# Dense-weight conversion in pairs of blocks: one 1024-column operation where two of 512 columns stood

## The chip, the cores and the metric

The kernel runs on one core of one Trainium2 chip. The time is the device time of one execution in microseconds, taken as the median of three runs.

## The reference

Three layers follow each other on 2304 tokens (4 sequences of 576) of width 512:

```
scores = q @ k.T / sqrt(64)           # 8 heads, causal, window of 64 keys
attn   = softmax(where(mask, scores, -1e9)); x = attn @ v
h = max(x @ w_in, 0);  x = (h * h) @ w_out        # dense: 512 -> 2048 -> 512
e = argmax(x @ w_gate); g = softmax(x @ w_gate)[e]  # 8 experts, one for each token
out = g * (max(x @ w1[e], 0) @ w2[e])             # 512 -> 1024 -> 512
```

In the program the two dense weight arrays `w_in` and `w_out` arrive as 64-bit words, two 32-bit words for each element; the kernel makes fp32 numbers of them.

## The kernel before

Matrix products are made of three products each: a number is kept as a high part (rounded to TensorE's fp32r format) and a low part (the rest), and `mm3` adds high by high, high by low and low by high (lines 168 to 170).

The dense layer works on 9 slices `st` of 256 tokens and 16 chunks `f` of 128 hidden columns. `gemm1(st, f)` makes a chunk's hidden values, `hidden` (ScalarE, L464), `square` (ScalarE L471, VectorE L473) and `square_low` (VectorE, L480) turn them into the parts `gh` and `gl`, and `gemm2(st, f)` adds them to the slice's output. A list `order` gives the pairs (st, f): slices 0 and 1 interleaved first, then slice after slice. Attention (`att_scores` to `att_out`) runs ahead, in blocks `g` of 64 tokens; the first eight blocks take their maxima straight from PSUM (L377) and scale them in a second operation (L380), before ScalarE's exponentials (L398).

The dense weights are converted while slices 0 and 1 run. A chunk f has two blocks of 128 x 512 elements, n = 2f from `w_in` and n = 2f+1 from `w_out`. The steps are:

- `load_w(n)` issues the DMA of one block (512 KB) from SyncE's queue into a ring `stg` of four buffers.
- `conv_a(f)`: ScalarE takes the absolute value of the upper words of each block (L186) into a ring `tmp` of four.
- `conv_b(f)`: four steps on VectorE for each block: clamp (L203), shift and mask (L205), merge with the sign and exponent bits (L207), merge with the lower word's bits (L211). Then it asks for the blocks of chunk f + 2.
- `conv_c(f)`: for each block ScalarE makes the high part (L228), and VectorE or GpSimd the low part (L230): VectorE every third block, GpSimd the others.

A table of slots says when each step is emitted; the order within an engine's queue in the dense part comes out of a planner that simulates the program with its own costs. After the dense part the experts' weights go through the same `stg` buffers (`wload`, `wsplit`), and each expert is one group of products.

Of the kernel before, what the change touches and what calls it, by code (L numbers as in the profile page):

```python
# [11 lines left out]
F32 = mybir.dt.float32  # L12
F32R = mybir.dt.float32r
BF16 = mybir.dt.bfloat16
I32 = mybir.dt.int32
U32 = mybir.dt.uint32
ACTF = mybir.ActivationFunctionType
ALU = mybir.AluOpType
AX = mybir.AxisListType
P = 128  # L20


def word(bits):

    return struct.unpack("<f", struct.pack("<I", bits))[0]
# [24 lines left out]
def kernel(  # L50
# [13 lines left out]
    nc = tc.nc  # L64
    B, _, NB, W, HP = qT.shape
# [3 lines left out]
    E, _, F1 = w1.shape  # L69
# [13 lines left out]
    SCALE = 1.0 / math.sqrt(D)  # L83
# [4 lines left out]
    cpool = ctx.enter_context(tc.tile_pool(name="cpool", bufs=1))  # L88
# [4 lines left out]
    bpool = bpool_ctx.__enter__()  # L93
# [3 lines left out]
    cr = Ring(cpool)  # L97
    br = Ring(bpool)
# [6 lines left out]
    kring = epool.tile([P, 4, HP, W], F32, tag="k", name="k")  # L105
    xhl = [epool.tile([P, KD, 3 * ST], F32R, tag=f"x{p_}", name=f"x{p_}") for p_ in "hl"]

    br.make([P, 512], I32, "tmp", 4)
    for p_ in "hl":
        br.make([P, ST], F32R, f"g{p_}", 3)  # L110

# [7 lines left out]
    for half in range(2):  # L119
# [5 lines left out]
            out=mid, in_=mid, pattern=[[-1, P]], compare_op=ALU.is_ge, fill=NEG, base=W, channel_multiplier=1  # L125
# [33 lines left out]
    def wunit():  # L159
        return cr.tile([P, 4096], F32R, "w", 4)  # L160
# [12 lines left out]

    wi_u, wo_u, wst = {}, {}, {}

    def stage():
        return cr.tile([P, 1024], F32, "stg", 4)


    conv = {}  # L180

    def conv_a(f):
        for n in (2 * f, 2 * f + 1):
            w = wst.pop(n).rearrange("p (n two) -> p n two", two=2)
            c = br.tile([P, 512], I32, "tmp", 4)
            nc.scalar.activation(c.bitcast(F32), w[:, :, 1].bitcast(F32), ACTF.Abs)  # L186
            conv[n] = w[:, :, 0], w[:, :, 1], c

    def conv_b(f):
        half, fo = divmod(f, NF // 2)  # L190
        if f == NF // 2:
            fpool_ctx.__exit__(None, None, None)
            wpool = ctx.enter_context(tc.tile_pool(name="wpool", bufs=1, side="right"))
            cr.tiles["w"] += [wpool.tile([P, 4096], F32R, tag=f"w{i}", name=f"w{i}") for i in range(4, 8)]
        if fo == 0:
            for p_ in "hl":
                wi_u[half, p_] = wunit().rearrange("p (k f) -> p k f", k=KD)
                wo_u[half, p_] = wunit().rearrange("p (f d) -> p f d", d=DM)
        two = [conv.pop(2 * f + i) for i in range(2)]

        for _, _, c in two:
            cf = c.bitcast(F32)
            nc.vector.tensor_scalar(cf, cf, word(0x38100000), word(0x47EFFFFF), op0=ALU.max, op1=ALU.min)  # L203
        for _, _, c in two:
            nc.vector.tensor_scalar(c, c, 3, 0x3FFFFFFF, op0=ALU.logical_shift_left, op1=ALU.bitwise_and)  # L205
        for _, high, c in two:
            nc.vector.scalar_tensor_tensor(  # L207
                out=c, in0=high, scalar=-(1 << 30), in1=c, op0=ALU.bitwise_and, op1=ALU.bitwise_or
            )
        for low, _, c in two:  # L210
            nc.vector.scalar_tensor_tensor(  # L211
                out=c, in0=low, scalar=29, in1=c, op0=ALU.logical_shift_right, op1=ALU.bitwise_or
            )
        conv[f, "c"] = two
        for n in (2 * f + 4, 2 * f + 5):
            if n < 2 * NF:
                load_w(n)

    def conv_c(f):
        half, fo = divmod(f, NF // 2)  # L220
        for which, (_, _, c) in enumerate(conv.pop((f, "c"))):
            c = c.bitcast(F32)
            if which:
                h, l = (wo_u[half, p_][:, fo, :] for p_ in "hl")
            else:
                h, l = (wi_u[half, p_][:, :, fo * P:(fo + 1) * P] for p_ in "hl")
                c = c.rearrange("p (k f) -> p k f", k=KD)
            nc.scalar.copy(h, c)  # L228
            low = nc.vector if (2 * f + which) % 3 == 2 else nc.gpsimd
            low.tensor_tensor(l, c, h.bitcast(F32), op=ALU.subtract)  # L230

    def load_w(n):
        f, which = divmod(n, 2)
        wst[n] = stage().bitcast(I32)
        if which:
            nc.sync.dma_start(wst[n], w_out[f * P:(f + 1) * P, :])
        else:
            nc.sync.dma_start(
                wst[n].rearrange("p (k f) -> p k f", k=KD),
                w_in[:, 2 * f * P:2 * (f + 1) * P].rearrange("(k p) f -> p k f", p=P),  # L240
            )
# [3 lines left out]
    wsp, stg, busiest, done = {}, {}, [], {}  # L245
# [127 lines left out]
    def att_max(g):  # L373
        ps = probs[g]
        if g < NE:
            nmax = br.tile([P, HP], F32, "nmax", 3)
            nc.vector.tensor_reduce(  # L377
                out=nmax, in_=ps.rearrange("p (h k) -> p h k", h=HP), axis=AX.X, op=ALU.max, negate=True
            )
            nc.vector.tensor_scalar_mul(nmax, nmax, SCALE)  # L380
            probs[g] = ps, nmax
            return
        s = er.tile([P, HP, P], F32, "s", 3)
        m = mask[:, 0 if g % NB else 1, :].unsqueeze(1).to_broadcast([P, HP, P])
        nc.vector.scalar_tensor_tensor(
            out=s, in0=ps.rearrange("p (h k) -> p h k", h=HP), scalar=SCALE, in1=m, op0=ALU.mult, op1=ALU.min
        )
        nmax = br.tile([P, HP], F32, "nmax", 3)
        nc.vector.tensor_reduce(out=nmax, in_=s, axis=AX.X, op=ALU.max, negate=True)
        probs[g] = s, nmax  # L390
# [463 lines left out]
    nc.vector.tensor_copy(ident_b, ident)  # L854
    nc.vector.tensor_scalar_min(mask_b, mask, 0.0)
    load_w(0)
    load_w(1)
    load_q(2, 2)
    load_k(2, 2)
# [35 lines left out]
    def chain(i, stages, x, gaps, most=2):  # L895
# [8 lines left out]
        return i  # L904

    ATT = (att_scores, att_max, att_exp, att_norm, att_transpose, att_evac, att_values, att_out)
    at(16, load_gates, 0)

# [6 lines left out]
    for f in range(NF):  # L915
        i = max(-3, min(f - 1, slot[0, f] - 2))
        at(i, conv_c, f)
        at(i - 1, conv_b, f)
        if f + 1 < NF:
            at(i - 1, conv_a, f + 1)  # L920
# [6 lines left out]
    for g in range(2 * QB, NS * QB):  # L927
        st, j = divmod(g, QB)
        i = slot[st, 0] - 19 + 4 * j
        if st == 2:  # L930
            i = slot[st, 0] - 13 + 2 * j
# [9 lines left out]
    for i in range(8):  # L941
# [3 lines left out]
        at(last + 8 + i, wload, *((-1, i + 4) if i < 4 else (0, i - 4)))  # L945

    conv_a(0)
    for i in range(-PRE, len(order) + LA):
        run(i, False)
# [5 lines left out]
        if i >= LA:  # L955
            st, f = order[i - LA]
# [200 lines left out]
```

## Time and profile before

| | |
|---|---|
| median of 3 runs | 841.28 us (840.61 to 845.0) |
| the profiled execution | 844.22 us, its span 842.5 us |
| PE busy | 789.9 us (94%) |
| DVE busy | 546.4 us (65%) |
| ACT busy | 400.6 us (48%) |
| POOL busy | 254.6 us (30%) |

PE is TensorE (PEld its weight loads), DVE is VectorE, ACT is ScalarE, POOL is GpSimd, SP is SyncE. Busy times are sums over instructions of one engine. The span is what the trace covers; the profiled execution's own time lies 1.7 us above it. The profiled execution is one of its own, beside the three runs.

### The profile page before, as it was taken

The numbers are of one execution on the slowest core, as the hardware profiler recorded it, in microseconds if no ns is written. First come the engines' busy times: TensorE is split into PE (matmuls) and PEld (weight loads), VectorE is DVE, ScalarE is ACT, GpSimd is POOL, SyncE is SP. The second block draws the span as 40 slices with busy tenths as digits, with TensorE's granted clock in tenths as the row PEclk, the third lists the DMA queues.
The fourth block names the chain that finished last, engine by engine and source line by source line (L and its number), as shares of the span: only waits on it lengthen the run. The fifth ranks groups of instructions, "written<-read, shape, count | busy, mean of one in ns | idle before, by whom it ended". The sixth has DMA issues, their size and how long they took to land.

```text
span 842.5 us, 15052 instructions
## 1 busy us (share of the span) xinstructions
PE 789.9 (94%) x5212; PEld 685.0 (81%) x5212; DVE 546.4 (65%) x1275; ACT 400.6 (48%) x1059; POOL 254.6 (30%) x257
## 2 busy tenths in 40 slices
PE   6888788999999999999999998989999999999894
PEld 5766667988889888889888897878798888888783
DVE  6999996795773946748558478557778654534110
ACT  6986654343443434344443435436677553433211
POOL 5425431112221122211211006164567642320201
PEclk9999999999999999999999999989999999999998
DMA  9854653110211212111110036366667654420101
GB/s 272 278 148 150 200 154 110 38 39 26 82 32 39 66 36 77 32 45 62 40 51 27 26 100 202 126 213 185 205 205 250 220 154 146 124 91 2 50 2 42
DMA packets 50861, 91.51 MB, mean 109 GB/s; under 512 B 8220, under 2 KB 24604, under 8 KB 50752
## 3 DMA queue, kind: packets, MB, share of 16 engines
q1 hardware_dynamic: 44688, 80.43, 30.3%
q0 software_dynamic: 6064, 9.63, 3.4%
q8 instruction: 69, 1.13, 0.5%
q14 instruction: 40, 0.33, 0.1%
HBM read 84.59 MB, written 13.81 MB: 117 GB/s over the span
## 4 chain that ended last, share of the span: by engine, by line
PE 64%; issue 14%; DVE 11%; DMA 6%; ACT 2%; POOL 2%; SPq 0%; POOLq 0%; DVEq 0%; ACTq 0%
PE h L168 10%; PE h L169 10%; PE h L170 10%; PE y L168 9%; PE y L170 9%; PE y L169 9%; DMA stg<-in_moe_w_out 2%; PE a L362 2%; DVE tmp L207 2%; DVE tmp L211 2%; PE a L435 2%; DVE tmp L203 1%; DMA stg<-in_moe_w 1%; PE a L685 1%; PE a L420 1%
## 5 line engine op out<-in xcount | busy, mean ns | idle before, releaser
L168 PE MATMUL h<-xh,w 128*128 128x256 f32 (+3 forms) x864 | 263.0, 305 | 18.4 <-DVE gl L480 14.2
L169 PE MATMUL h<-xl,w 128*128 128x256 f32 (+3 forms) x864 | 254.9, 295 | 0.4 <-DVE xl L997 0.4
L170 PE MATMUL h<-xh,w 128*128 128x256 f32 (+3 forms) x864 | 254.6, 295 | 0.0
L168 PEld LDWEIGHTS h<-xh,w 128*128 128x128 f32 x864 | 164.2, 190 | 37.9 <-DVE gl L480 19.5
L169 PEld LDWEIGHTS h<-xl,w 128*128 128x128 f32 x864 | 164.5, 190 | 8.1 <-DVE xl L997 0.6
L170 PEld LDWEIGHTS h<-xh,w 128*128 128x128 f32 x864 | 164.4, 190 | 2.8
L464 ACT ACTIVATE r<-h 128x256 f32<-128x256 f32 x144 | 55.2, 384 | 201.7 <-PE h L170 194.0
L168 PE MATMUL y<-w,gh 128*128 128x512 f32 x294 | 119.2, 406 | 4.0 <-ACT gh L471 3.9
L772 DVE SCALAR_TENSOR_TENSOR ggl<-h,ggh 128x512 fp32r<-128x512 f32 (+1 forms) x69 | 46.2, 669 | 114.2 <-ACT ggh L771 114.1
L169 PE MATMUL y<-w,gh 128*128 128x512 f32 x294 | 116.4, 396 | 0.0
L473 DVE SCALAR_TENSOR_TENSOR h<-h,r 128x256 f32<-128x256 f32 x144 | 61.3, 426 | 84.4 <-ACT r L464 84.4
L170 PE MATMUL y<-w,gl 128*128 128x512 f32 x294 | 102.3, 395 | 0.5 <-DVE gl L772 0.5
L771 ACT ACTIVATE ggh<-h 128x512 fp32r<-128x512 f32 (+1 forms) x69 | 40.3, 584 | 124.6 <-PE h L170 96.0
L550 DVE SCALAR_TENSOR_TENSOR tmp<-tmp,stg 128x512 f32<-128x512 f32 x128 | 95.6, 747 | 0.8
L336 POOL COPY q<-qd 64x256 f32<-64x256 f32 x46 | 33.5, 729 | 149.7 <-PE a L362 148.4
L168 PE MATMUL y<-w,ggh 128*128 128x512 f32 x170 | 70.8, 416 | 0.6 <-ACT ggh L771 0.6
L170 PE MATMUL y<-w,ggl 128*128 128x512 f32 x170 | 67.6, 398 | 1.4 <-DVE junk L998 1.1
L168 PEld LDWEIGHTS y<-w,gh 128*128 128x128 f32 x294 | 55.6, 189 | 15.4 <-ACT gh L471 6.0
L169 PE MATMUL y<-w,ggh 128*128 128x512 f32 x170 | 67.1, 395 | 0.0
L480 DVE TENSOR_TENSOR gl<-h,gh 128x256 fp32r<-128x256 f32 x144 | 60.4, 420 | 7.7 <-ACT gh L471 1.0
L278 POOL TENSOR_TENSOR w<-stg,w 128x512 fp32r<-128x512 f32 x27 | 36.4, 1354 | 91.6 <-ACT w L277 88.7
L169 PEld LDWEIGHTS y<-w,gh 128*128 128x128 f32 x294 | 55.6, 189 | 9.5
(165 smaller groups left out, 1276.1 us busy)
## 6 DMA issues: line engine op xcount, KB each, us to landing
stg<-in_moe_w SPq DMA_DIRECT2D x45, 512.0 KB, 4.1
stgx<-in_moe_w SPq DMA_DIRECT2D x18, 512.0 KB, 4.5
stg<-in_moe_w_in SPq DMA_DIRECT2D x16, 512.0 KB, 4.3
stg<-in_moe_w_out SPq DMA_DIRECT2D x16, 512.0 KB, 3.9
v<-in_v SPq DMA_DIRECT2D x28, 256.0 KB, 2.6
x_d<-tmp SPq DMA_DIRECT2D x18, 256.0 KB, 2.0
q<-in_moe_w SPq DMA_DIRECT2D x9, 512.0 KB, 4.7
qd<-in_q SPq DMA_DIRECT2D x28, 128.0 KB, 2.1
```

The lines of the kernel that those rows point to most:

```text
L168: nc.tensor.matmul(o, lhsT=ah, rhs=bh, start=first, stop=False)
L169: nc.tensor.matmul(o, lhsT=ah, rhs=bl, start=False, stop=False)
L170: nc.tensor.matmul(o, lhsT=al, rhs=bh, start=False, stop=last)
L207: nc.vector.scalar_tensor_tensor(out=c, in0=high, scalar=-(1 << 30), in1=c, op0=ALU.bitwise_and, op1=ALU.bitwise_or)
L278: rest.tensor_tensor(l[:, a:a + 512], src, h[:, a:a + 512].bitcast(F32), op=ALU.subtract)
L336: nc.gpsimd.tensor_copy(qk[g][rows, :, half, :], d[rows])
L464: nc.scalar.activation(r, gT[st, f][:, :ST], ACTF.Relu)
L473: nc.vector.scalar_tensor_tensor(out=ps[:, ST:2 * ST], in0=ps[:, :ST], scalar=0.0, in1=r, op0=ALU.max, op1=ALU.mult)
L480: nc.vector.tensor_tensor(gl, ps[:, ST:2 * ST], gh.bitcast(F32), op=ALU.subtract)
L550: nc.vector.scalar_tensor_tensor(out=junk, in0=x2sb[tt], scalar=1.0, in1=w, op0=ALU.mult, op1=ALU.mult, accum_out=l[:, t, e:e + 1])
L771: nc.scalar.activation(h[:, :width], hid[f][:, :width], ACTF.Relu)
L772: nc.vector.scalar_tensor_tensor(out=l[:, :width], in0=hid[f][:, :width], scalar=0.0, in1=h[:, :width].bitcast(F32), op0=ALU.max, op1=ALU. ...
```

## The change

The rings `tmp` and `stg` become pairs: two tiles of twice the size each, whose halves are the old four buffers. `conv_a` takes the absolute value of a chunk's two blocks in one operation of 1024 columns, and the four steps of `conv_b` are one operation each on 1024 columns. `conv_c` still works on the halves; of the low parts VectorE now makes every sixth (five of 32), GpSimd the others. The scaling of the first eight maxima goes from VectorE to ScalarE.

```
-    br.make([P, 512], I32, "tmp", 4)
+    tmp2 = [bpool.tile([P, 2, 512], I32, tag=f"tmp{i}", name=f"tmp{i}") for i in range(2)]
+    br.tiles["tmp"], br.at["tmp"] = [t[:, i] for t in tmp2 for i in range(2)], -1
+    stg2 = [cpool.tile([P, 2, 1024], F32, tag=f"stg{i}", name=f"stg{i}") for i in range(2)]
+    cr.tiles["stg"], cr.at["stg"] = [t[:, i] for t in stg2 for i in range(2)], -1
...
     def conv_a(f):
-        for n in (2 * f, 2 * f + 1):
-            w = wst.pop(n).rearrange("p (n two) -> p n two", two=2)
-            c = br.tile([P, 512], I32, "tmp", 4)
-            nc.scalar.activation(c.bitcast(F32), w[:, :, 1].bitcast(F32), ACTF.Abs)
-            conv[n] = w[:, :, 0], w[:, :, 1], c
+        i = (br.at["tmp"] + 1) % 4
+        assert i % 2 == 0
+        c = [br.tile([P, 512], I32, "tmp", 4) for _ in range(2)]
+        whole = tmp2[i // 2].rearrange("p t n -> p (t n)")
+        w = stg2[f % 2].bitcast(I32).rearrange("p t (n two) -> p (t n) two", two=2)
+        nc.scalar.activation(whole.bitcast(F32), w[:, :, 1].bitcast(F32), ACTF.Abs)
+        conv[f] = w[:, :, 0], w[:, :, 1], whole, c
...
-        two = [conv.pop(2 * f + i) for i in range(2)]
-        for _, _, c in two:
-            cf = c.bitcast(F32)
-            nc.vector.tensor_scalar(cf, cf, word(0x38100000), word(0x47EFFFFF), op0=ALU.max, op1=ALU.min)
...
+        low, high, c, _ = conv[f]
+        cf = c.bitcast(F32)
+        nc.vector.tensor_scalar(cf, cf, word(0x38100000), word(0x47EFFFFF), op0=ALU.max, op1=ALU.min)
+        nc.vector.tensor_scalar(c, c, 3, 0x3FFFFFFF, op0=ALU.logical_shift_left, op1=ALU.bitwise_and)
+        nc.vector.scalar_tensor_tensor(
+            out=c, in0=high, scalar=-(1 << 30), in1=c, op0=ALU.bitwise_and, op1=ALU.bitwise_or
+        )
+        nc.vector.scalar_tensor_tensor(
+            out=c, in0=low, scalar=29, in1=c, op0=ALU.logical_shift_right, op1=ALU.bitwise_or
+        )
...
-            low = nc.vector if (2 * f + which) % 3 == 2 else nc.gpsimd
+            low = nc.vector if (2 * f + which) % 6 == 5 else nc.gpsimd
...
-            nc.vector.tensor_scalar_mul(nmax, nmax, SCALE)
+            nc.scalar.mul(nmax, nmax, SCALE)
```

## Rows read from the trace of the kernel before

**Rows 1.** Stages: us, then busy us (instructions) by engine, clock, DMA share, GB/s

```profile
0.00:44.00 44.00, 32.98 (x265) 29.37 (x266) 36.72 (x83) 35.81 (x111) 21.19 (x38) 0.96 0.86 266
44.00:137.50 93.50, 75.91 (x520) 61.05 (x520) 92.09 (x176) 59.57 (x152) 36.02 (x28) 0.98 0.51 159
137.50:490.00 352.50, 352.50 (x2595) 312.96 (x2594) 226.88 (x700) 146.61 (x476) 67.02 (x78) 1.00 0.15 46
490.00:842.00 352.00, 328.47 (x1838) 281.63 (x1836) 190.71 (x320) 158.57 (x323) 130.34 (x114) 0.97 0.43 139
```

**Rows 2.** The chain that ended last, its shares by engine

```profile
PE 64%; issue 14%; DVE 11%; DMA 6%; ACT 2%; POOL 2%; SPq 0%; POOLq 0%; DVEq 0%; ACTq 0%
```

**Rows 3.** Waits from 44 to 137.5 us: total us, times, longest us

```profile
PEld h L168 <- DVE gl L480: 16.5, 17, 2.2
PE h L168 <- DVE gl L480: 12.6, 12, 1.8
...
ACT tmp L186 <- DMA stg<-in_moe_w_in: 5.8, 4, 4.6
...
ACT tmp L186 <- DMA stg<-in_moe_w_out: 4.7, 5, 1.5
...
ACT tmp L186 <- DVE w L230: 3.6, 3, 2.0
...
DVE tmp L203 <- ACT tmp L186: 1.4, 2, 0.9
```

**Rows 4.** VectorE's groups from 44 to 137.5 us: busy us, mean ns, idle before

```profile
L207 DVE SCALAR_TENSOR_TENSOR tmp<-stg,tmp 128x512 int32<-128x512 int32 x24 | 19.6, 819 | 0.0
L211 DVE SCALAR_TENSOR_TENSOR tmp<-stg,tmp 128x512 int32<-128x512 int32 x24 | 19.6, 816 | 0.0
L205 DVE TENSOR_SCALAR tmp<-tmp 128x512 int32<-128x512 int32 x24 | 16.8, 705 | 0.0
L203 DVE TENSOR_SCALAR tmp<-tmp 128x512 f32<-128x512 f32 x24 | 13.0, 542 | 1.4 <-ACT tmp L186 1.4
...
L230 DVE TENSOR_TENSOR w<-tmp,w 128x512 fp32r<-128x512 f32 x8 | 7.0, 872 | 0.0
```

**Rows 5.** VectorE in order of time from 63 us: start, duration

```profile
63.13 0.16 DVE L412 TENSOR_SCALAR tot<-tot 128x4 f32<-128x4 f32 x1
63.20 0.42 DVE L205 TENSOR_SCALAR tmp<-tmp 128x512 int32<-128x512 int32 x1
63.53 0.41 DVE L165 TENSOR_TENSOR xl<-a,xh 128x256 fp32r<-128x256 f32 x1
...
64.20 0.69 DVE L207 SCALAR_TENSOR_TENSOR tmp<-stg,tmp 128x512 int32<-128x512 int32 x1
64.80 0.42 DVE L480 TENSOR_TENSOR gl<-h,gh 128x256 fp32r<-128x256 f32 x1
```

**Rows 6.** GpSimd's groups from 44 to 137.5 us

```profile
L230 POOL TENSOR_TENSOR w<-tmp,w 128x512 fp32r<-128x512 f32 x16 | 23.1, 1446 | 40.6 <-ACT w L228 40.6
L414 POOL TENSOR_TENSOR s<-s,tot 128x512 f32<-128x512 f32 x6 | 7.7, 1278 | 11.3 <-DVE tot L413 11.2
L336 POOL COPY q<-qd 64x256 f32<-64x256 f32 x6 | 6.7, 1117 | 7.9 <-PE a L362 7.7
```

**Rows 7.** GpSimd in order of time near 81 us

```profile
80.73 1.49 POOL L414 TENSOR_TENSOR s<-s,tot 128x512 f32<-128x512 f32 x1
```

**Rows 8.** VectorE in order of time, beside rows 7

```profile
81.25 0.41 DVE L165 TENSOR_TENSOR xl<-a,xh 128x256 fp32r<-128x256 f32 x1
81.58 0.93 DVE L205 TENSOR_SCALAR tmp<-tmp 128x512 int32<-128x512 int32 x1
82.42 0.42 DVE L473 SCALAR_TENSOR_TENSOR h<-h,r 128x256 f32<-128x256 f32 x1
```

**Rows 9.** ScalarE's conversion groups, 44 to 137.5 us

```profile
L186 ACT ACTIVATE tmp<-stg 128x512 f32<-128x512 f32 x22 | 14.8, 674 | 16.6 <-DMA stg<-in_moe_w_in 5.8 <-DMA stg<-in_moe_w_out 4.7 <-DVE w L230 3.6
```

**Rows 10.** Loads of stg issued from 44 to 137.5 us, issue to landing

```profile
DMA to landing us min/median/max: 3.2/3.7/6.4
```

**Rows 11.** The scaling of the first eight maxima: ns min/median/max, first and last start

```profile
L380 DVE TENSOR_SCALAR nmax<-nmax x8: 155/158/999, 8.9 to 34.7; 128x4 f32<-128x4 f32 x8
```

More of the change, by code (lines that the diff above doesn't have):

```diff
@@ L174 @@
     wi_u, wo_u, wst = {}, {}, {}
-    def stage():
-        return cr.tile([P, 1024], F32, "stg", 4)
     conv = {}
     def conv_a(f):
-        for n in (2 * f, 2 * f + 1):
-            w = wst.pop(n).rearrange("p (n two) -> p n two", two=2)
-            c = br.tile([P, 512], I32, "tmp", 4)
-            nc.scalar.activation(c.bitcast(F32), w[:, :, 1].bitcast(F32), ACTF.Abs)
-            conv[n] = w[:, :, 0], w[:, :, 1], c
+        i = (br.at["tmp"] + 1) % 4
[5 more added lines that the diff above has]
+        conv[f] = w[:, :, 0], w[:, :, 1], whole, c
     def conv_b(f):
@@ L198, in conv_b @@
                 wo_u[half, p_] = wunit().rearrange("p (f d) -> p f d", d=DM)
-        two = [conv.pop(2 * f + i) for i in range(2)]
-        for _, _, c in two:
-            cf = c.bitcast(F32)
-            nc.vector.tensor_scalar(cf, cf, word(0x38100000), word(0x47EFFFFF), op0=ALU.max, op1=ALU.min)
[L204 to L214, printed above, removed]
+        low, high, c, _ = conv[f]
[8 more added lines that the diff above has]
+        )
         for n in (2 * f + 4, 2 * f + 5):
@@ L220, in conv_c @@
         half, fo = divmod(f, NF // 2)
-        for which, (_, _, c) in enumerate(conv.pop((f, "c"))):
+        for which, c in enumerate(conv.pop(f)[3]):
             c = c.bitcast(F32)
@@ L233, in load_w @@
         f, which = divmod(n, 2)
-        wst[n] = stage().bitcast(I32)
+        wst[n] = cr.tile([P, 1024], F32, "stg", 4).bitcast(I32)
         if which:
```

## The prediction

> **What bounds the kernel now.** I read the stages first, then the chain that ended last, then the waits of the one stage that the change touches, and last VectorE and GpSimd there in order of time.
>
> The stages [rows 1] show three regimes. From 137.5 to 490 us PE is busy for the whole 352.5 us: what arrives at its start late ends late, and nothing that VectorE or ScalarE does faster inside it matters. From 490 us on PE has 24 us of gaps, among the experts' groups, which the change doesn't touch. From 44 to 137.5 us VectorE is busy for 92.1 of 93.5 us, and PE only for 75.9: VectorE is the bound, and PE has 17.6 us of gaps to give back. These 93.5 us hold the conversion of 12 of the 16 chunks (24 instructions of each step [rows 4]), 7.8 us a chunk. Before 44 us loads are the pace: the DMA engines are busy for 86% at 266 GB/s, VectorE for 36.7 of 44 us.
>
> The chain agrees: VectorE holds 11% of the span, some 93 us, beside PE's 64% [rows 2]. In the waits PE's first product of a chunk and its weight load wait for L480, the low part of the hidden values, 12.6 and 16.5 us (much of it the same time) [rows 3]. L480 itself is short; it stands in VectorE's queue behind the conversions. So a microsecond less of VectorE work between 44 and 137.5 us should bring the fully busy stretch of PE forward by about a microsecond, and the end with it.
>
> In order of time one sees two things. First, a spacing: a 512-column clamp or shift takes 0.33 us from its start to the next, a merge of two operands 0.60 us, and an operation on 4 columns still takes 0.07 us [rows 5]. Second, a stall: GpSimd's L414 runs from 80.73 to 82.22 us [rows 7]; VectorE's L165, which reads PSUM, passes beside it in its usual 0.41 us, but the next operation, L205, which reads and writes SBUF alone, takes 0.93 us instead of 0.42 and ends 0.29 us after GpSimd [rows 8]. The conversions carry this all through: mean 0.819, 0.816, 0.705, 0.542 and 0.872 us [rows 4] against 0.69 and 0.42 undisturbed [rows 5]. Times the counts this is 3.1 + 3.0 + 6.8 + 2.9 + 1.5 = 17.3 us of stall in the stage, while GpSimd works for 23.1 + 7.7 + 6.7 = 37.5 us [rows 6].
>
> **The change, part by part.** The sum goes by the profiled execution (844.22 us) as a difference, and I put the difference on the median of the runs, 841.28 us; the profiled one lies 2.9 us above it, inside the spread of the three.
>
> *Merged steps on VectorE.* An operation of 1024 columns instead of two of 512 saves one fixed part, 0.07 us [rows 5]. From 44 to 137.5 us that is 12 chunks x 4 x 0.07 = 3.4 us, on the engine that bounds. The four earlier chunks save 1.1 us, and I count them as nothing: there the loads are the pace.
>
> *Low parts to GpSimd.* Five go over (n = 2, 8, 14, 20, 26), four of them in the stage. VectorE is rid of 4 x 0.60 = 2.4 us. GpSimd gets 4 x 1.446 = 5.8 us more [rows 6]; it has the room (36.0 of 93.5 us busy), but its work stalls VectorE. By busy time a low part's share of the stall is 23.1/37.5 x 17.3 / 16 = 0.67 us, and 0.81 if the copies L336 cost nothing. On that count moving is worth 4 x (0.67 - 0.60) = +0.3 us, so nothing. Against that, stalls need an SBUF operation next in VectorE's queue: the conversions are 104 of its 176 instructions [rows 1, 4], and after merging 52 of 124, 0.71 of the former share. If stalls fall like it, they are 17.3 x 43.3/37.5 x 0.71 = 14.2 us, 3.1 less, and with the 2.4 the gain is 5.5 us. Neither end is shown; I take about their middle, -2.6 us. The upper bound of the cost is a stall for GpSimd's whole operation: 4 x (1.446 - 0.60) = +3.4 us.
>
> The row shows GpSimd's operation holding up VectorE only from the first SBUF operation on [rows 7, 8]. The Trainium skill, page "SBUF — State Buffer", sections "SBUF: two separate sides" and "Summary: rules for kernel authors", says that the two share a port pair as an exclusive lock held for the whole instruction, that a VectorE operation in a two-port mode or with two SBUF inputs is blocked fully, and that one should schedule whichever is off the critical path. Taken at its full length it speaks against moving low parts, and the sum would be -3.4 + 3.4 + 1.4 = +1.4 us instead of -4.6; the mean stall above, about half of an operation, bears out the lock but not its full length.
>
> *The pair as the unit.* ScalarE's absolute value now needs both blocks landed and both halves of `tmp` free, VectorE's clamp needs all of it, and both loads of chunk f + 2 are asked for at the end of one operation. Behind a waiting L186 stand ScalarE's L464, L471 and the exponentials, for which VectorE (L473, L480) and PE wait; behind the two loads in SP's queue stand those of k, q and v. Now ScalarE waits 5.8 + 4.7 us for blocks and 3.6 us for a low part, and VectorE only 1.4 us for ScalarE [rows 3]. After VectorE's last step the chain is: load, 3.7 us (6.4 at the longest) [rows 10], for the second block 0.52 MB at 266 GB/s = 2.0 us more, then some 1.2 us of ScalarE for twice 0.674 [rows 9]. That is 6.9 us, against the 7.4 us that VectorE will want for the other chunk and all else. The cover is there but thin. I put VectorE's waits at twice the former, +1.4 us; bounds are nothing and what the first rival says.
>
> *ScalarE.* 16 operations fewer, eight scalings more: with 59.6 of 93.5 us busy it is no bound in the stage. The scalings fall before 35 us [rows 11], where it is busy for 35.8 of 44 us. VectorE loses 8 x 0.07 = 0.6 us there. Hidden behind the loads, both ways: 0; bounds -0.6 and, if nothing hid ScalarE's eight and each took 0.4 us, as VectorE's steps on 256 columns do [rows 8], +3.
>
> The sum: -3.4 - 2.6 + 1.4 = -4.6 us: 841.28 - 4.6 = **836.7 us**. Its own range is -2 to -7.5 us.
>
> **Rivals.** *Loads set the pace (slower).* The pair lands later: 6.4 us for the first and 0.52 MB at the stage's 159 GB/s, 3.3 us, for the second, with 1.2 us of ScalarE 10.9 us, 3.5 us beyond the 7.4. Then VectorE idles before L203, or ScalarE before L186 with the hidden values behind it. For it: ScalarE already waits for blocks nine times [rows 3]. Against: half of the DMA time is free [rows 1], and other VectorE work can fill holes. At 1.0 us a chunk: -6.0 + 12 = +6 us, 847.3 us. A mean wait of 0.5 us a chunk eats the gain; above 0.85 us the kernel is slower by over 0.5%.
>
> *GpSimd's work costs its full length (no change).* Moved low parts at +3.4 us undo the merging, -3.4 + 3.4 + 1.4 = +1.4 us, 842.7 us. For it: a queue of long SBUF operations leaves little of GpSimd's time beside work on PSUM; against: the mean of 0.67 of 1.446.
>
> *More comes back.* Stalls fall by share, and the early chunks count: -3.4 - 5.5 - 1.1 - 0.6 - 0.6 (the low part n = 2) = -11.2 us, 830.1 us. For it: VectorE is busy for 36.7 of the first 44 us too; against: the load pace there [rows 1].
>
> **How the numbers follow.** The forecast gets 0.50, the lost gain by loads 0.18, the full lock 0.14, the larger gain 0.18. 0.5% of 841 us is 4.2 us, about what a measurement of this kernel can tell from no change. Of the forecast's range a bit over half lies beyond it, so faster is 0.27 + 0.18 = 0.45; slower is most of the first rival, 0.17; the rest, 0.38, is within 0.5%. The range of 8 in 10 reaches from the larger gain, 831 us, to beyond the full lock, 844 us; it leaves out the tail of the first rival.
>
> **What the profile after would show.** Right: VectorE still busy for nearly all of a stage that ends some 4 us earlier; L203 and L205 at about 0.6 us apart undisturbed and L207 and L211 at about 1.13; 27 low parts on GpSimd at about 1.4 us; PE waiting less for L480; everything after shifted. Wrong: idle time of VectorE before L203, released by L186 or by the loads; ScalarE's idle time before L186 well above 16.6 us; stalls over 20 us in the stage; or PE gaps that come back in the experts' part. The planner's order is not in the trace, and another order that puts waiting operations ahead of ready ones would also make it wrong.

## The result, and the profile after

The changed kernel takes 833.17 us (median of 4 runs, 832.06 to 834.53), the kernel before beside it 841.92 us (4 runs, 840.61 to 845.0): a ratio of 0.9893, interval 0.9877 to 0.9909, that is 8.75 us or 1.1% faster. A second set gave 0.9909 (0.9889 to 0.9929). The forecast was 836.7 us in a range of 831 to 844, faster with a chance of 0.45: the side and the range hold, but the gain is nearly twice the forecast and lies beyond the narrower range of the sum itself (-2 to -7.5 us).

The stages of the kernel after; here VectorE's last conversion step ends at 130.6 us and not at 137.5, so the stage from 44 us is cut at 131:

```profile
0.00:44.00 44.00, 32.62 (x242) 28.10 (x242) 30.55 (x58) 35.71 (x113) 23.00 (x38) 1.00 0.83 255
44.00:131.00 87.00, 79.20 (x564) 66.88 (x562) 85.63 (x127) 58.31 (x144) 48.49 (x32) 0.96 0.52 176
```

Columns as in [rows 1]. VectorE (the third pair) is still busy for nearly the whole stage, 85.6 of 87.0 us; the stage is 6.5 us shorter. PE's gaps in it fall from 17.6 to 7.8 us, though the first 44 us are as they were (33.0 against 32.6 us of PE).

A mark that every trace has is the issue of the first slice's output (the first `x_d` write in SyncE's queue). Up to it every kernel but one has done the same 901 products. The stages from 0 to that mark, before and after:

```profile
0.00:155.61 155.61, 127.00 (x901) 106.91 (x902) 134.89 (x272) 101.45 (x278) 59.64 (x67) 0.98 0.57 177
```

```profile
0.00:145.57 145.57, 126.39 (x901) 108.33 (x902) 121.01 (x195) 99.43 (x270) 74.04 (x72) 0.98 0.58 190
```

The mark moves from 155.6 to 145.6 us. TensorE does the same work in 127.0 and 126.4 us; its gaps fall from 28.6 to 19.2 us. VectorE's busy time falls by 13.9 us, 77 instructions fewer. From there the traces run in parallel: the last slice is written out at 536.8 and 526.1 us. The spans, 842.5 and 829.9 us, differ by 2 us more, but that is scatter among the experts: 305.7 us from the last slice to the end before, 303.8 after, and 308.7 in a second trace of the kernel before. The spans differ by more than the times, because the profiled executions of the kernel before (844.22 and, in the second trace, 845.64 us) lie 2.9 and 3.5 us above the medians of their runs, those of the kernel after (832.06 and 833.56 us) within 1.1 us of theirs.

VectorE's groups from 44 to 131 us in the kernel after (L205, L206, L207, L210 are the four steps, L228 the low part):

```profile
L207 DVE SCALAR_TENSOR_TENSOR tmp<-stg,tmp 128x1024 int32<-128x1024 int32 x12 | 18.6, 1553 | 0.0
L210 DVE SCALAR_TENSOR_TENSOR tmp<-stg,tmp 128x1024 int32<-128x1024 int32 x13 | 17.4, 1338 | 0.0
L206 DVE TENSOR_SCALAR tmp<-tmp 128x1024 int32<-128x1024 int32 x12 | 12.8, 1066 | 0.0
L205 DVE TENSOR_SCALAR tmp<-tmp 128x1024 f32<-128x1024 f32 x12 | 11.2, 934 | 0.3 <-ACT tmp L189 0.2
...
L228 DVE TENSOR_TENSOR w<-tmp,w 128x512 fp32r<-128x512 f32 x4 | 4.7, 1164 | 0.0
```

And VectorE in order of time, where two of them run undisturbed:

```profile
116.68 1.21 DVE L210 SCALAR_TENSOR_TENSOR tmp<-stg,tmp 128x1024 int32<-128x1024 int32 x1
117.81 0.41 DVE L478 TENSOR_TENSOR gl<-h,gh 128x256 fp32r<-128x256 f32 x1
118.15 0.68 DVE L205 TENSOR_SCALAR tmp<-tmp 128x1024 f32<-128x1024 f32 x1
118.75 0.42 DVE L471 SCALAR_TENSOR_TENSOR h<-h,r 128x256 f32<-128x256 f32 x1
```

A merge on 1024 columns takes 1.13 us to the next start and a clamp 0.60, against twice 0.60 and twice 0.33 [rows 5]: 0.07 and 0.06 us saved each. Against 1.21 and 0.68 undisturbed (0.69 for the low part), the groups carry 4.1 + 1.7 + 4.6 + 3.0 + 1.9 = 15.3 us of stall; before it was 17.3 [rows 4]. In a second trace of each kernel the same count gives 14.3 us after and 15.1 before, so a fall of 2 us is no more than two traces of one kernel differ by. GpSimd's groups in the same stretch:

```profile
L228 POOL TENSOR_TENSOR w<-tmp,w 128x512 fp32r<-128x512 f32 x20 | 33.1, 1670 | 19.3 <-ACT w L226 19.2
L412 POOL TENSOR_TENSOR s<-s,tot 128x512 f32<-128x512 f32 x6 | 8.3, 1385 | 12.3 <-DVE tot L411 12.3
L334 POOL COPY q<-qd 64x256 f32<-64x256 f32 x6 | 7.4, 1229 | 5.3 <-PE a L360 5.1
```

Twenty low parts now instead of sixteen [rows 6], and each longer (1.670 against 1.446 us). That GpSimd in its turn waits behind VectorE's operations of 1.2 us is likely, not shown; its last two low parts, which run when VectorE's conversion is over, take 2.54 us together, 1.27 each. The waits of the stage after, as in [rows 3]:

```profile
ACT tmp L189 <- DMA stg<-in_moe_w_out: 9.8, 6, 2.5
...
PEld h L172 <- DVE gl L478: 6.0, 6, 1.6
...
PE h L172 <- DVE gl L478: 3.4, 6, 1.1
...
ACT tmp L189 <- POOL w L228: 1.9, 1, 1.9
...
DVE tmp L205 <- ACT tmp L189: 0.2, 1, 0.2
```

TensorE's products wait 3.4 us for the hidden values' low part where they waited 12.6 (3.8 and 9.6 in the second traces). ScalarE waits 9.8 us for the pair of blocks, about what it waited for both before, and VectorE waits 0.2 us for ScalarE: the longer unit stays covered. Loads of `stg` in the stage, issue to landing:

```profile
DMA to landing us min/median/max: 3.7/4.5/5.0
```

### The profile page after: what moved, and what is told of

It reads as the page before. It is cut to its first block, busy times and chain, and to the rows that moved or that the text cites. A ratio compares the mean times of both kernels' runs of the same rounds, so it can differ in the third digit from the quotient of the medians.

```text
span 829.9 us, 14957 instructions
## 1 busy us (share of the span) xinstructions
PE 787.3 (95%) x5212; PEld 685.5 (83%) x5212; DVE 530.4 (64%) x1198; ACT 398.8 (48%) x1051; POOL 269.9 (33%) x262
## 3 DMA queue, kind: packets, MB, share of 16 engines
q8 instruction: 69, 1.13, 0.6%
## 4 chain that ended last, share of the span: by engine, by line
PE 66%; issue 13%; DVE 9%; DMA 5%; ACT 4%; POOL 1%; ACTq 0%; SPq 0%; POOLq 0%; DVEq 0%
PE h L172 11%; PE h L173 10%; PE h L174 10%; PE y L172 10%; PE y L174 9%; PE y L173 9%; PE a L360 2%; DMA stg<-in_moe_w_out 2%; PE a L433 2%; PE a L418 1%; DVE tmp L205 1%; DVE tmp L210 1%; PE a L683 1%; DVE tmp L207 1%; DMA out<-s,tab 1%
## 5 line engine op out<-in xcount | busy, mean ns | idle before, releaser
L471 DVE SCALAR_TENSOR_TENSOR h<-h,r 128x256 f32<-128x256 f32 x144 | 61.4, 426 | 84.0 <-ACT r L462 84.0
L478 DVE TENSOR_TENSOR gl<-h,gh 128x256 fp32r<-128x256 f32 x144 | 60.5, 420 | 8.3 <-ACT gh L469 1.5
```

Of the source, the lines that this page charges most:

```text
L471: nc.vector.scalar_tensor_tensor(out=ps[:, ST:2 * ST], in0=ps[:, :ST], scalar=0.0, in1=r, op0=ALU.max, op1=ALU.mult)
L478: nc.vector.tensor_tensor(gl, ps[:, ST:2 * ST], gh.bitcast(F32), op=ALU.subtract)
```

## Experiments

The marks below come from one trace of each kernel; how far a mark scatters is told by the first two runs.

**Both kernels again.** No edit.

> The kernel before, unchanged, as a run of its own: a second trace and a second set of times. If a kernel's dense part repeats and the scatter of the times is made among the experts, the first slice of the dense layer is written out at 155.6 us again, within 0.3 us, the last at 536.8, and only the time after that moves by some us. If the dense part itself scatters, these marks move by 2 us and more.

> The changed kernel, unchanged, as a run of its own. If the dense part repeats, its first slice is written out at 145.6 us and its last at 526.1 again, within 0.3 us, 10.0 and 10.7 us ahead of the kernel before. The ratio of times should again be about 0.989; if a good part of the difference was the luck of few runs, it is 0.993 or more.

Before: 842.16 us, ratio to itself 0.9995 (0.998 to 1.0011), marks 155.2 and 535.2 us. After: 833.37 us, 0.9909 (0.9889 to 0.9929), marks 146.7 and 526.7 us. The first mark repeats within 1.1 us, less well than I had written (0.3), so the gain at the first mark is 8.5 to 10.0 us. From the last slice to the end of the span the kernel before has 305.7 and 308.7 us, and over all traces with the same experts' work it is 303.4 to 309.3 us: much of the scatter of the times lies among the experts, and a mark leaves it out.

**One part alone.** Three kernels: the changed one with two edits undone, and the one before with one edit each.

```
merge_only (from after):  low = nc.vector if (2 * f + which) % 3 == 2 else nc.gpsimd
                          nc.vector.tensor_scalar_mul(nmax, nmax, SCALE)
low_only   (from before): low = nc.vector if (2 * f + which) % 6 == 5 else nc.gpsimd
nmax_only  (from before): nc.scalar.mul(nmax, nmax, SCALE)
```

> The changed kernel with the low parts shared as before (VectorE every third block) and the maxima scaled on VectorE as before: only the pairs and the merged operations are left. Theory A (the fixed parts of the merged steps, with VectorE's bound relieved): 4 x 16 x 0.07 = 4.5 us less VectorE work, so 3.5 to 5 us faster than before. Theory B (the gain comes from fewer stalls behind GpSimd, since fewer separate VectorE operations on SBUF are there to be caught): stalls between 44 us and the end of conversion fall from 17.3 to some 13 us, and the kernel is 7 to 9 us faster than before.

> The kernel before with one edit: VectorE makes every sixth low part instead of every third, five more go to GpSimd. If a low part on GpSimd stalls VectorE for about as long as VectorE would have needed for it (0.67 to 0.81 us against 0.60), there is no change: -1 to +1 us. If it stalls VectorE for its whole length (1.4 us), +3 to +4 us. If the move is worth VectorE's own time, -2.4 to -3 us.

> The kernel before with one edit: the first eight maxima are scaled on ScalarE. Theory: the first 35 us are paced by loads, so no change, -0.6 to +0.5 us. Rival: the scaling on VectorE was caught behind GpSimd (one of the eight took 0.999 us) and delays the exponentials, so that 1 to 3 us come back.

**Two parts of three.** The changed kernel with the maxima back on VectorE, and with the low parts shared as before.

```
merge_low  (from after): nc.vector.tensor_scalar_mul(nmax, nmax, SCALE)
merge_nmax (from after): low = nc.vector if (2 * f + which) % 3 == 2 else nc.gpsimd
```

> The changed kernel with the maxima scaled on VectorE as before: merged steps and moved low parts. Marks of the dense part so far: before 155.6 and 155.2, changed 145.6 and 146.7, merged steps alone 148.0, moved low parts alone 155.9. Additive: 148 +- 1 us and about 837 us. If moving pays only once the steps are merged, so that few separate operations are there to be stalled, 146 us or earlier and about 834 us.

> The changed kernel with the low parts shared as before (VectorE every third): merged steps and the maxima on ScalarE. If the move of the low parts is worth nothing, this is the changed kernel again, mark 145.5 to 147 us, ratio to before 0.989 to 0.992. If the move carries a part, mark 148 us or later and a ratio of 0.994 or more. Together with the changed kernel (five low parts on VectorE) and the one with none it makes a series of 10, 5 and 0.

**No low part on VectorE.** The changed kernel with `low = nc.gpsimd`.

> The changed kernel with all 32 low parts on GpSimd instead of 27. If stalls cost what VectorE would need itself, the same as the changed kernel within 1.5 us. If moving is worth VectorE's own 0.60 us each, 2 to 3 us faster than the changed kernel. If GpSimd becomes late for TensorE (low parts of both blocks of a chunk in a row, 3 us), 2 to 6 us slower than the changed kernel, with waits of TensorE for the low parts.

| kernel | ratio to before (interval) | first slice out, us | VectorE busy until then, us | stall until the last conversion step, us |
|---|---|---|---|---|
| before, two traces | 1; 0.9995 (0.998 to 1.0011) | 155.6; 155.2 | 134.9; 134.1 | 23.0; 21.1 |
| merge_only | 0.9957 (0.9934 to 0.9979) | 148.0 | 124.5 | 17.7 |
| low_only | 1.0022 (1.0005 to 1.0039) | 155.9 | 134.4 | 24.4 |
| nmax_only | 0.9999 (0.9975 to 1.0023) | 152.5 | 134.1 | 19.4 |
| merge_low | 0.9954 (0.9937 to 0.9972) | 149.4 | 126.3 | 21.7 |
| merge_nmax | 0.9923 (0.9907 to 0.9938) | 148.5 | 126.3 | 18.0 |
| after, two traces | 0.9893 (0.9877 to 0.9909); 0.9909 (0.9889 to 0.9929) | 145.6; 146.7 | 121.0; 121.4 | 18.7; 17.2 |
| all_pool | 0.9991 (0.9971 to 1.0011) | 152.5 | 123.3 | 22.9 |

The last column counts stall as in the section before (0.69 and 0.42 us undisturbed for single steps, 1.21 and 0.68 for merged ones), from the start of the trace. For merge_only the groups of the stage, from 44 to 133.1 us, are:

```profile
L210 DVE SCALAR_TENSOR_TENSOR tmp<-stg,tmp 128x1024 int32<-128x1024 int32 x13 | 17.1, 1316 | 0.0
L207 DVE SCALAR_TENSOR_TENSOR tmp<-stg,tmp 128x1024 int32<-128x1024 int32 x12 | 16.6, 1382 | 0.0
L206 DVE TENSOR_SCALAR tmp<-tmp 128x1024 int32<-128x1024 int32 x12 | 12.0, 1001 | 0.0
L205 DVE TENSOR_SCALAR tmp<-tmp 128x1024 f32<-128x1024 f32 x12 | 9.8, 816 | 0.8 <-ACT tmp L189 0.8
...
L228 DVE TENSOR_TENSOR w<-tmp,w 128x512 fp32r<-128x512 f32 x8 | 9.3, 1161 | 0.4 <-ACT w L226 0.4
```

What follows for the merged steps. They are in every kernel that gains, and alone (merge_only) they bring the mark forward by 7 us and VectorE's work down by 10 us: more than the 4.5 us of fixed parts (theory A). The rest goes with less stall. In the stage alone it is 12.7 us, near the 13 of theory B, but there the count scatters (17.3 and 15.1 in the two traces of the kernel before, 13.3 in nmax_only, 15.0 in merge_nmax). Over the whole conversion it separates: each kernel with merged steps has less stall than every kernel with single steps and the same number of low parts on VectorE (17.7 and 18.0 against 19.4 to 23.0 with ten, 17.2 to 21.7 against 24.4 with five). In time it is otherwise: 3.6 us better is what theory A forecast, and the 7 to 9 us of theory B lie outside the interval. Nearly 4 us of the gain at the mark don't arrive in the times. A part may lie in the executions that were profiled: those of the kernel before took 2.9 and 3.5 us more than its median, that of merge_only (838.14 us) about its median. How much isn't shown.

For the other two parts. Moving low parts with single steps is worth nothing or a little less (+1.9 us, mark unchanged), as the count by busy time had it. On merged steps alone it is worth nothing either (merge_low against merge_only: the same time, the mark 1.4 us later, 4.0 us more stall); so merging by itself doesn't make the move pay, which one of the expectations held possible. On top of merged steps and ScalarE's maxima the changed kernel is 2 to 3 us ahead of merge_nmax at the mark and 1.2 to 2.5 us in time, but the intervals of the ratios overlap: that this part carries is not shown. Taking the last five away as well loses 6 to 8 us again. The maxima alone make no difference in time, though the mark comes 2.7 to 3.1 us earlier, with as much VectorE work as in the second trace of the kernel before (134.1 us). On merged steps and moved low parts they bring 3 to 5 us; on merged steps alone some 3 us of time (the intervals overlap) and nothing at the mark. So the parts don't add: 3.6 - 1.9 + 0.1 us against 7.7 to 9. The order in every queue is a new one with each edit, and that is worth as much as one of the small parts; what makes the 4 to 5 us of time by which the changed kernel is ahead of merge_only, order or stall, stays open.

In all_pool VectorE's merged steps in the stretch from 44 to 137.5 us show where the limit of moving is:

```profile
L207 DVE SCALAR_TENSOR_TENSOR tmp<-stg,tmp 128x1024 int32<-128x1024 int32 x13 | 21.7, 1669 | 0.0
L210 DVE SCALAR_TENSOR_TENSOR tmp<-stg,tmp 128x1024 int32<-128x1024 int32 x13 | 17.9, 1374 | 0.0
L206 DVE TENSOR_SCALAR tmp<-tmp 128x1024 int32<-128x1024 int32 x12 | 14.0, 1164 | 0.0
L205 DVE TENSOR_SCALAR tmp<-tmp 128x1024 f32<-128x1024 f32 x12 | 13.0, 1080 | 1.8 <-ACT tmp L189 1.8
```

By the same count this is 18.7 us of stall, 3.4 more than after. The four low parts that VectorE makes there in the kernel after cost it 4.7 us with their stalls; without them its sum doesn't fall but is 2 us higher at the mark (123.3 against 121.0 and 121.4 us), and its idle time until there is 4 us longer (29.2 against 24.6 and 25.3). It waits 1.8 us for ScalarE, 1.6 of them right behind an absolute value that had waited for a low part of GpSimd to free `tmp`; ScalarE's waits for loads are longer too (13.1 us, 9.8 in the kernel after). The kernel is 7 to 8 us slower than the changed one, more than the 2 to 6 of the expected line, and not by the waits of TensorE on low parts that this line named: they are 1.1 us at most, against 1.5 in the kernel after. Which of these changes makes the 7 us isn't shown.

**The stall taken away.** The changed kernel without the low parts of the dense weights; their tiles are filled with zero once for each half of the chunks.

```
+            for l in (wi_u[half, "l"], wo_u[half, "l"]):
+                nc.gpsimd.memset(l.bitcast(F32), 0.0)
-            low.tensor_tensor(l, c, h.bitcast(F32), op=ALU.subtract)
```

> The changed kernel without the dense weights' low parts: the 32 subtractions are left out, and the tiles of the low parts are filled with zero once by four long writes on GpSimd, so the products lose that part and the output isn't the reference's. Theory (stalls are GpSimd's): the four merged steps show 0.69 and 1.21 us nearly everywhere, stalls in the stage fall from 15.3 us to 5 us or less (what scaling of the attention rows and copies of q leave), VectorE's work in the stage falls by 10 us for these and 2.4 us for its own low parts, and the conversion ends 8 to 12 us earlier, unless loads or TensorE stop it before. Rival (long durations are the operations' own, by form or place): they stay at 0.93 to 1.55 us in the mean.

VectorE's groups from 44 to 126 us, where the conversion ends (L207, L208, L209, L212 are the four steps here), then VectorE and GpSimd in order of time near 56 us:

```profile
L212 DVE SCALAR_TENSOR_TENSOR tmp<-stg,tmp 128x1024 int32<-128x1024 int32 x12 | 16.1, 1344 | 0.0
L207 DVE TENSOR_SCALAR tmp<-tmp 128x1024 f32<-128x1024 f32 x12 | 15.7, 1311 | 3.1 <-ACT tmp L189 3.0
L209 DVE SCALAR_TENSOR_TENSOR tmp<-stg,tmp 128x1024 int32<-128x1024 int32 x12 | 14.8, 1233 | 0.1
L208 DVE TENSOR_SCALAR tmp<-tmp 128x1024 int32<-128x1024 int32 x12 | 9.2, 770 | 0.1
```

```profile
55.79 7.37 DVE L207 TENSOR_SCALAR tmp<-tmp 128x1024 f32<-128x1024 f32 x1
```

```profile
55.63 6.98 POOL L203 MEMSET w<- 128x4096 f32 x2 [7.31 <-DMA qd<-in_q]
```

One clamp stood 7.37 us beside the two writes that I had put in, and makes 6.7 of the 7.5 us by which L207 exceeds 0.69 us. The other three carry 1.6 + 0.3 + 1.0 = 2.9 us instead of 10.4 with low parts. So the long durations do come from GpSimd, not from the operations. Without the clamp that my writes held, 3.7 us of stall are left of 15.3, so the twenty low parts on GpSimd cost VectorE some 0.58 us each (with the 1.9 us by which they held up its own four). The gain in time that I expected isn't there: the ratio is 0.9951 (0.9933 to 0.997) and the mark 149.0 us. The writes for the first half ran at 2.75 us for 6.96 us, ahead of a part of attention's masks in GpSimd's queue, VectorE's first work on hidden values (L471) came at 47.0 us instead of 38.5, and TensorE was busy for 25.4 instead of 32.6 of the first 44 us. From that first L471 to the mark it takes 102.0 us against 107.1. The conversion ended at 125.7 us, 4.9 earlier, not the 8 to 12 expected: VectorE was busy for 77.3 of 81.7 us and waited 3.0 us for ScalarE, 2.8 of them right behind absolute values that had waited for a block. Loads had begun to count.

**Order.** Both kernels with the conversion of later chunks up to four slots later.

```
-        i = max(-3, min(f - 1, slot[0, f] - 2))
+        i = max(-3, min(f - 1 + max(0, f - 6) // 2, slot[0, f] - 2))
```

> The kernel before with one edit: chunk f of the dense weights is converted up to four slots later (one more for every second chunk from 8 on), with no operation changed. Theory C (a part of the gain is order: the conversions were taken ahead of the hidden values that TensorE waits for, and 18.1 us of TensorE's work was left when they ended): TensorE's waits for L480 fall, and the first slice is written out 2 to 6 us earlier than at 155.6 us although VectorE does the same work. Rival (only VectorE's total counts): no change within 1 us, or later, as TensorE then waits for weights.

> The changed kernel with the same later slots. Theory C: the changed kernel has 14.6 us of TensorE's work left when conversion ends, so there is still 1 to 4 us to be had, first slice out at 142 to 144.5 us. Rival: no change within 1 us of 145.6, or 1 to 4 us later, as the weights of the last chunks come too late.

In these two the gate's weights are loaded into `stg` buffers whose last dense blocks are not yet converted: two absolute values in before_late and one merge in after_late wait for `stg<-in_gates`. The last chunks are then made of other numbers and the tokens are routed otherwise, so everything behind the dense part is another program (979.79 and 972.02 us), and only the marks are read. Before: 155.4 us, as without the edit, and TensorE's products wait 12.3 us for L480, as without it (12.6 and 9.6). After: 149.2 us, later by 2.5 to 3.6, though TensorE's products wait only 2.5 us for L478; its planner also put 15 more products ahead of the mark, 916 instead of 901. So these later slots gain nothing. As they didn't shorten the waits in the kernel before, they don't settle whether order carries a part of the gain; nmax_only, with its mark 2.7 us ahead at the same 134.1 us of VectorE, says that VectorE's sum is not all that counts.

**The copies of q on ScalarE.** The changed kernel with one number changed in `lay_q`:

```
-            if g < NE + 5:
+            if g < NE + 11:
```

> The changed kernel with one edit: for six more blocks of attention, those of the conversion stage, the copies of q are made by ScalarE and not by GpSimd. By the stalls after the copies, 12 operations of 0.6 us net that stall little, -0.5 to -2 us at the mark of the first slice (144 to 145.5 us), and a ratio to before of 0.986 to 0.989. If ScalarE, with 58 of 87 us busy, becomes late for the hidden values: 0 to +2 us.

835.56 us, 0.9935 (0.9909 to 0.996), mark 146.5 us with 121.3 us of VectorE: the changed kernel again at the mark, and no better in time. The stall from 44 us on is 15.5 us, as with the copies on GpSimd (15.3 and 14.3): the copies of 64 partitions by 256 columns weren't what stalled VectorE. No version that was run beats the changed kernel.

## Why the prediction came out as it did

*VectorE bounds the conversion stage, and PE's gaps are what can be had.* Right. It is busy for 92.1 of 93.5 us before and 85.6 of 87.0 after, TensorE's 901 products take the same time, and its gaps shrink. The forecast's range holds, and the sum was too small, by the step that follows and by the low parts.

*A microsecond of VectorE brings TensorE forward by about a microsecond.* Too little. The stage ends 6.5 us earlier, and the mark moves by 10.0 us (5.3 and 8.5 in the second pair of traces). In the shorter stage VectorE did two more of the operations of L471 (22 against 20), and TensorE was further: some 806 of its 901 products were done at the end of the stage, against 785. So it had 14.6 us left instead of 18.1. Why the hidden values came forward against the conversions isn't shown; the queues' order is the likely reason.

*Merged steps, -3.4 us.* Right for the fixed parts: 0.06 to 0.07 us each, 3.1 to 3.4 us for 12 chunks. That merging also lowers the stall stood under the low parts; merge_only shows that it does without any low part moved.

*Low parts, -2.6 us between -5.5 and +0.3.* The sign held in the traces, for another reason than the move. VectorE's own time falls by 2.4 us, and the stall by 2.0 in spite of four more low parts on GpSimd, -4.4 us; in the second pair of traces the stall falls by 0.8, -3.2 us. Either fall of stall is within what two traces of the kernel before differ by (17.3 and 15.1). It came near the share that I had worked out (14.2 us predicted for that end, 15.3 and 14.3 measured). By busy time a low part on GpSimd costs VectorE 33.1/48.8 x 15.3/20 = 0.52 us with merged steps, against 0.67 before; if the copies cost nothing, as after_q_act has it, it is 33.1/41.4 x 15.3/20 = 0.61 us against 0.81, and taking the low parts away gives 0.58. That is about VectorE's own 0.60 us: the move by itself was worth nothing (low_only, merge_low), and what fall of stall there is goes with the merging (merge_only).

*The pair as the unit, +1.4 us.* Mis-sized: nothing. VectorE's idle time in the stage is 1.4 us in both kernels. The cover that I called thin held: the pair landed at the latest 5.0 us after issue, where I had put 5.7 for the second block.

These terms make -3.4 - 4.4 + 0 = -7.8 us at the upper count of the merging, and the three more operations of L471 and L478 (22 + 22 against 20 + 21, 0.33 us each) take 1.0 back: -6.8 us, where the stage shows -6.5. That this closes so well is in part luck: the fall of stall in it is no larger than the scatter.

*ScalarE's scalings and the first 44 us, 0.* As far as one can tell right for progress there: VectorE has 6.2 us less work in the first 44 us and is idle for that much longer, and TensorE's busy time is the same, with a few products fewer done (242 against 265). That the maxima cost nothing and bring nothing holds for the time of nmax_only (0.9999), not for its mark (2.7 to 3.1 us earlier) and not in combination (3 to 5 us).

The rivals: loads as the pace is refuted for the changed kernel by 0.2 us of waits; its beginning shows where VectorE has less to do (nolow_after, 3.0 us of waits). The full lock length as the mean price is refuted by some 0.6 us for an operation of 1.670, and by merge_low, which is no slower than merge_only. The result lies between my forecast and the rival with the larger gain (830.1 us), which had the stall about right and the early chunks wrong.

The Trainium skill (page "SBUF — State Buffer", section "SBUF: two separate sides") describes the port pair of VectorE and GpSimd as a lock held for a whole instruction. The traces agree in that VectorE's stall falls from 15.3 to 3.7 us when GpSimd's low parts are taken away (nolow_after), and that one clamp was held until GpSimd's writes were over.

## What to carry to other kernels

Where VectorE and GpSimd share SBUF, count two things for an engine that bounds: the fixed part of each instruction, and how many separate instructions stand ready to be caught behind the other engine. Merging operations cut both here, and the second was of the size of the first (4.2 us of fixed parts over the whole conversion, 1.4 to 5.3 of stall). Price a move to GpSimd by its share of the stall in the trace, not by its duration, and try more than one split: with 10, 5 and 0 low parts left the mark came at 148.5, 145.6 to 146.7 and 152.5 us, where only the last is clear of noise in time.

When a run's times scatter by some microseconds, a mark early in the trace, with the same work done up to it, can tell small edits apart that the total can't. Read it beside the total: a mark here repeats within 1.1 us at best, and nmax_only has one 3 us earlier without being faster.

## What was unexpected

Two writes of 128 x 4096 by GpSimd in a row held one VectorE clamp for 7.37 us, through both of them, 6.98 us; between two low parts in a row VectorE got a turn, in the place that was read (in the kernel after two run for 3.05 us from 118.62 us, and a shift of VectorE that starts at 119.08 us takes 1.45 us). And parts that make +1.9, 0 and -3.6 us alone make -8 us together.
